# An attention and double feed-forward kernel: weight blocks placed by when their room comes free, stores in another queue, slots taken from two ends, and a new order at the end of phase one

## The chip, the cores and the metric

The kernel runs on one core of a Trainium2 chip. Five engines work side by side, each through its own instructions in order: TensorE (PE, matrix products), VectorE (DVE), ScalarE (ACT), GpSimd (POOL) and SyncE (SP, which here only issues transfers). Transfers run on 16 DMA engines and are issued from the queue of SP, ACT or POOL. The metric is the device time of one execution in microseconds (us); lower is better.

## What is computed

The input is q, k and v of 8 batches, 8 heads, 576 positions and 64 elements. Attention runs inside chunks of 64 positions; its result, 4608 tokens of 512 elements, goes through two feed-forward layers:

```python
def _moe_ref(x, w_in, w_out, g_ln):              # 512 -> 1024 -> 512
    h = x @ w_in
    h_max = np.max(h, axis=-1, keepdims=True)
    e = np.exp(h - h_max)
    sm = e / (np.sum(e, axis=-1, keepdims=True) + 1e-09)
    solu = h * sm
    mu = np.mean(solu, axis=-1, keepdims=True)
    var = np.mean((solu - mu) ** 2, axis=-1, keepdims=True)
    ln = (solu - mu) / np.sqrt(var + 1e-06) * g_ln
    return (ln @ w_out).astype(np.float32)

def _moe2_ref(x, w_in, w_out, alpha):            # 512 -> 2048 -> 512
    h = x @ w_in
    g = np.maximum(h, 0.0) + alpha * np.minimum(h, 0.0)
    return (g @ w_out).astype(np.float32)
```

## The kernel before

All arithmetic is in float32 accuracy. PE multiplies each operand as a high and a low part, so each product is three matmuls: high by high, high by low, low by high.

**Phase one** (`phase1`) does attention and the first layer on 36 tiles of 128 tokens. Its instructions stand in an order written out by hand: `FIRST`, `STEP` (repeated for each tile) and `LAST` (from line 81). In these lists `zt35` is the set of transposes of tile 35 on PE, `zh35` and `zl35` its high part (ACT) and low part (DVE), `ya31` and `yb31` the two halves of tile 31's product with `wo` on PE (24 matmuls each, lines 162 to 164), `ye31` the evacuation of that product by ACT into `ysb` and its store to DRAM (`yd`), and `sy0` to `sy7` are steps of phase two's preparation. Entries that have been done already are skipped; of `LAST`'s first line `ya30 yb30 ye29` have. The product lies in one PSUM buffer until `LAST` begins, where a second one is added, so ya31 needs ye30 out of the way; from there tiles take the two buffers in turn.

**Phase two** (`phase2`) is the second layer, with 7 products in place of 8 for a product of matrices of two by two blocks (p1 to p7 of `PRODUCTS`). Its **first half** goes through 6 groups s of 2 x 384 tokens, and in each through 8 units b, one for each weight block. A unit (class `Unit`, function `unit`) makes 7 products of 6 matmuls (line 764), adds them on DVE, applies the activation on ACT and DVE, and leaves four tiles 22, 11, 12 and 21 in g buffers, of which there are 6 for all units. `store` (line 807) sends each to DRAM (`gd`): in group 0 from POOL's queue, later from SP's. Tiles 12 and 21 of a unit are stored in the next one (`late`). A unit takes its g buffers by turns, so tile 12 of a unit takes the buffer of tile 22 of the unit before.

Weight blocks are tiles of 1.8 MB. Blocks 0 and 1 lie in a pool of the left side and are loaded during phase one. Blocks 2 to 7 lie in one pool `w2r` (line 876) on the right side, in ascending order from the address where the first layer's `wo_h` and `wo_l` lie; 2 and 3 are loaded before the first unit and 4 to 7 in units 0 to 3 of group 0 (`extra`, k = 1). In group 5 the second half's weights take their places.

The input y of a group is loaded by `load_y` (line 722) in unit 0 of the group before (at k = 3), as four tiles; `sum_y` makes four sums of them on POOL (two instructions each), at units 1 to 4, and `high_y` and `low_y` split them on ACT and DVE. These tiles lie in 26 **slots** of one pool: `slot` takes the one that has been free longest, `free` puts it back.

The **second half** goes through chunks of tokens (`CHUNKS`), each in pieces j = 0 to 3 for the products p1, p5, p6, p7 and then for p2, p3, p4. `load_g` (line 897) loads a piece from `gd` (tiles a, b, c, d), `prepare` splits it on ACT and DVE, `multiply` does 12 matmuls for each product (line 961). Pieces 0 and 1 lie in the slots of the first half (names `fa`, `fhi` and so on), later ones in a pool of their own opened behind them (`ra`, `rhi`). Piece j reads weight blocks 2j and 2j + 1, so piece 3 needs blocks 6 and 7.

Each queue issues in the order of the program: an instruction that waits holds all that stands behind it on its engine, a store or a load too.

Of the kernel before, what the change touches and what calls it, by code (L numbers as in the profile page):

```python
# [9 lines left out]
F32 = mybir.dt.float32  # L10
F32R = mybir.dt.float32r
# [22 lines left out]
SG = 384  # L34
# [8 lines left out]
def order(text):  # L43
# [36 lines left out]
)  # L80
LAST = order(
    """
    zh34 zl34 ya30 yb30 ye29 zt35 zh35 zl35 ye30 ya31 yb31 sy0 ye31 ya32 yb32 sy1 sy2 ye32 ya33 yb33 sy3 sy4
    ye33 ya34 yb34 sy5 sy6 ye34 ya35 yb35 sy7 ye35
    """
)

# [2 lines left out]
def tile_chunk_attention_solu_prelu(  # L90
# [593 lines left out]
    def phase2():  # L684
        with ExitStack() as c2:
# [4 lines left out]
            wl = P("w2l", 1)  # L690
            ps2 = [P("ps_2l", 1, space=PSUM)]
            ca = c2.enter_context(ExitStack())
            tp = P("t2", 1, stack=ca)
            up = P("u2", 1, stack=ca)
            wr = None
            W, raw, th, tl = {}, {}, {}, {}

            def load_w(b, src):
                W[b] = (wl if b < NL else wr).tile([128, 2, 7, 256], F32R, name=f"w2{b}", tag=f"w{b}")
                if src is wi_dram:  # L700
                    nc.sync.dma_start(
                        out=W[b].bitcast(F32).rearrange("p t i c -> p (t i c)"),
                        in_=src[:, b].rearrange("p t i k c -> p (t i k c)"),
                    )
                else:
                    nc.sync.dma_start(out=W[b].bitcast(F32), in_=src[:, b])

            slots = [f"y{i}" for i in range(26)]  # L710
            homes = {}

            def slot(dtype, name):
                k = slots.pop(0)
                t = tp.tile([128, 2, SG], dtype, name=name, tag=k)
                homes[t.name] = k
                return t

# [1 line left out]
                slots.append(homes.pop(t.name))  # L720

            def load_y(s):
                for t in ("11", "12", "22", "21"):
                    r, c = int(t[0]) - 1, int(t[1]) - 1
                    raw[t] = slot(F32 if t == "12" else F32R, f"y{t}")
                    nc.sync.dma_start(
                        out=raw[t].bitcast(F32), in_=y_dram[s][:, 2 * r:2 * r + 2, SG * c:SG * c + SG]
                    )

            def sum_y(k):  # L730
                out, a, b = (("t3", "22", "12"), ("t1", "12", "11"), ("t2", "22", "t1"), ("t4", "21", "t2"))[k]
                raw[out] = raw["12"] if out == "t1" else slot(F32, f"y{out}")
                for h in range(2):
                    sub(nc.gpsimd, *(raw[x][:, h].bitcast(F32) for x in (out, a, b)))

            def high_y(s, p):
                t = PRODUCTS[p][1]
                th[s, t] = slot(F32R, "th")
                copy(th[s, t], raw[t].bitcast(F32))

            def low_y(s, p):
                t = PRODUCTS[p][1]
                h, f = th[s, t], raw[t]
                l = slot(F32R, "tl") if t[0] == "t" else f
                sub(nc.vector, l, f.bitcast(F32), h.bitcast(F32))
                if t[0] == "t":
                    free(f)
                th[s, t], tl[s, t] = h, l

            class Unit:  # L750
# [54 lines left out]
                    )  # L805

                def store(self, t):
                    eng = nc.gpsimd if self.s == 0 else nc.sync
                    eng.dma_start(out=GD[t][:, self.b, self.s * SG:self.s * SG + SG], in_=self.g[t])

                def late(self, k):

# [60 lines left out]
            yield  # L873
            nal_sb = P("sm2", 1, side="right").tile([128, 48], F32, name="nal")[:, 0:KF2]
            nc.gpsimd.tensor_scalar(out=nal_sb, in0=al_sb, scalar1=-1.0, scalar2=None, op0=ALU.mult)
            wr = P("w2r", 1, side="right")
            ps2.append(P("ps_2r", 1, side="right", space=PSUM))
            gp = P("g2", 1, side="right", stack=ca)
            for b in range(NL, NL + 2):
# [5 lines left out]
            steps = [(c, g, j, p) for c in range(len(CHUNKS)) for g in range(2) for j in range(4) for p in GROUPS[g]]  # L885
            pieces = [(c, g, j) for c in range(len(CHUNKS)) for g in range(2) for j in range(4)]
            start = {x: next(t for t, y in enumerate(steps) if y[:3] == x) for x in pieces}
            src, t4s, ops = {}, {}, {}

            def new(x, tag, dtype=F32R):  # L890
                n = CHUNKS[x[0]][1]
                if x in pieces[:2]:
                    return slot(dtype, f"f{tag}")
                bufs = dict(t3=1, t2=1, t4=4, hi=4, lo=3).get(tag, 2)
                return rp.tile([128, 2, 512], dtype, name=f"r{tag}", tag=tag, bufs=bufs)[:, :, :n]

            def load_g(x):
                c, g, j = x
# [52 lines left out]
            def multiply(t):  # L951
                c, g, j, p = steps[t]
                n = CHUNKS[c][1]
                i, _, key = PRODUCTS[p]
                hi, lo = ops.pop(((c, g, j), p))
                for m in range(2):
                    if j == 0 and p not in CHAINED:
                        bank[key, m] = ps2[m].tile([128, 512], F32, name=f"o{key}", tag=f"b{key}")
                    for k in range(2):
                        for q, (a, d) in enumerate(((0, hi), (0, lo), (1, hi))):  # L960
                            nc.tensor.matmul(  # L961
                                bank[key, m][:, :n], W[2 * j + k][:, a, i, 128 * m:128 * m + 128], d[:, k],
                                start=(p not in CHAINED and j + k + q == 0), stop=(j == 3 and k == 1 and q == 2),
                                skip_group_check=True,
                            )
# [41 lines left out]


            early = {(4, 1): "p1", (5, 1): "p6", (6, 1): "p5", (7, 1): "p7", (7, 3): "p2", (8, 0): "p3", (8, 1): "p4"}
            sums = {(1, 0): 0, (2, 0): 1, (3, 0): 2, (4, 0): 3}  # L1010
            prev = None
            for s in range(NS):
                for b in range(NB2):
                    def extra(k):
                        if s == 0 and k == 1 and NL + 2 + b < NB2:
                            load_w(NL + 2 + b, wi_dram)
                        if s + 1 == NS:
                            if (b, k) == (0, 3):
                                load_g(pieces[0])
                            if (b, k) == (7, 1):  # L1020
                                load_g(pieces[1])
                            if (b, k) in ((4, 2), (5, 2), (6, 2), (7, 0)):
                                prepare(pieces[0], GROUPS[0][b - 4])
                        else:
                            if (b, k) == (0, 3):
                                load_y(s + 1)
                            if (b, k) in sums:
                                sum_y(sums[b, k])
                            if (b, k) in early:
                                high_y(s + 1, early[b, k])  # L1030
                            if (b, k - 1) in early:
                                low_y(s + 1, early[b, k - 1])
# [8 lines left out]
                        load_w(b, wo_dram)  # L1041
            for k in range(3):
                prev.late(k)
            load_w(6, wo_dram)
            for p in GROUPS[0]:
                prepare(pieces[1], p)
            for t in range(8):
                multiply(t)
            ca.close()

            rp = P("g3", 2)
            op = P("o3", 1)
            LEAD = 3
            load_g(pieces[2])
            load_w(7, wo_dram)
            load_g(pieces[3])
            for t in range(8, 8 + LEAD):
# [45 lines left out]
```

## Time and profile before

| | |
|---|---|
| time, median of 3 runs | 1335.01 us (1334.02 to 1336.84) |
| the profiled execution | 1335.51 us |
| its span in the trace | 1333.7 us |
| PE busy | 1269.7 us, 95% |
| DVE / ACT / POOL busy | 948.2 / 689.7 / 344.6 us |
| end of phase one (its last matmul starts) | 601.10 us |
| group 0 of phase two | 601.22 to 674.67 us |
| turn to the second half | about 993 us |

The span is the time from the first to the last instruction in the trace; the time contains 1.8 us around it. The clock that PE was granted is given as a share of full speed (1.00 is 2.4 GHz, 0.50 is 1.2 GHz) and is a mean over the stretch. PE is the bound, so what matters is where it stands still or runs at the lower level, and which engine, store or load it waits for there.

### The profile page before, as it was taken

What the parts mean: (1) busy time and instruction counts of PE and PEld (TensorE: products, weight loads), DVE (VectorE), ACT (ScalarE), POOL (GpSimd) and SP (SyncE); (2) the same over time, 40 slices, a digit from 0 to 9 for tenths busy, and PEclk for the clock granted to TensorE, in tenths of its full rate; (3) what the DMA queues carried; (4) which work ended last, traced back from release to release, by engine and by line L of the source; (5) the groups of instructions that cost most, each with busy time, mean ns of one, the idle gap of its engine ahead of it and who ended that gap; (6) DMA issues with size and microseconds to landing.
All of it is one profiled execution on the core that took longest, in us unless ns stands there. A gap on an engine that the chain in (4) does not pass through costs nothing. (4 is left out here: it accounts for less than half of the span.)

```text
span 1333.7 us, 21442 instructions
## 1 busy us (share of the span) xinstructions
PE 1269.7 (95%) x7968; PEld 1168.9 (88%) x7968; DVE 948.2 (71%) x1425; ACT 689.7 (52%) x1140; POOL 344.6 (26%) x343
## 2 busy tenths in 40 slices
PE   4999899999999999997999999999989999999998
PEld 3778799999898889896999999999979888888898
DVE  6996586677767677423777777777766977868584
ACT  5685355555555654423566666666544444444443
POOL 4564154354645653322340202020000000000000
PEclk9799999999999999989999999999999999999999
DMA  9774267575757563339342424426986827466362
GB/s 234 174 169 118 68 174 178 149 173 170 212 160 214 186 187 103 138 131 382 147 153 109 154 109 151 151 110 215 345 293 210 277 95 268 143 220 206 132 232 95
DMA packets 212936, 237.87 MB, mean 178 GB/s; under 512 B 89312, under 2 KB 170720, under 8 KB 210784
## 3 DMA queue, kind: packets, MB, share of 16 engines
q1 hardware_dynamic: 200832, 219.98, 53.0%
q10 hardware_dynamic: 9792, 9.44, 2.1%
q0 software_dynamic: 2208, 7.08, 1.4%
q8 instruction: 63, 1.03, 0.3%
q14 instruction: 41, 0.34, 0.1%
HBM read 149.68 MB, written 86.77 MB: 177 GB/s over the span
## 5 line engine op out<-in xcount | busy, mean ns | idle before, releaser
L162 PE MATMUL yps<-zh,wo_h 128*128 128x256 f32 x576 | 168.7, 293 | 1.6 <-ACT ysb L588 1.6
L803 DVE SCALAR_TENSOR_TENSOR g<-ng,nal,g 128x384 f32<-128x384 f32 x192 | 124.4, 648 | 62.4 <-ACT g L682 62.4
L164 PE MATMUL yps<-zh,wo_l 128*128 128x256 f32 x576 | 164.2, 285 | 0.0
L163 PE MATMUL yps<-zl,wo_h 128*128 128x256 f32 x576 | 164.1, 285 | 0.0
L682 ACT ACTIVATE ng<-g 128x384 f32<-128x384 f32 x144 | 75.7, 526 | 147.9 <-DVE g L676 147.9
L764 PE MATMUL hv<-th,w 128*128 128x384 f32 x384 | 114.6, 339 | 12.7 <-DVE g L676 12.5
L764 PE MATMUL hz<-th,w 128*128 128x384 f32 x384 | 113.6, 336 | 5.7 <-DVE wv L676 5.7
L764 PE MATMUL hx<-th,w 128*128 128x384 f32 x384 | 113.7, 336 | 0.2 <-ACT s L682 0.2
L162 PEld LDWEIGHTS yps<-zh,wo_h 128*128 128x128 f32 x576 | 111.5, 194 | 1.9 <-ACT ysb L588 1.8
L163 PEld LDWEIGHTS yps<-zl,wo_h 128*128 128x128 f32 x576 | 111.5, 194 | 0.1
L164 PEld LDWEIGHTS yps<-zh,wo_l 128*128 128x128 f32 x576 | 111.2, 193 | 0.0
L961 PE MATMUL ox<-rhi,w 128*128 128x512 f32 (+1 forms) x304 | 94.8, 373 | 0.0
L961 PE MATMUL oz<-rhi,w 128*128 128x512 f32 (+1 forms) x304 | 93.8, 369 | 0.8 <-DVE osb L676 0.8
L961 PE MATMUL ov<-rhi,w 128*128 128x512 f32 (+1 forms) x304 | 93.7, 369 | 0.0
L682 ACT ACTIVATE rhi<-rt 128x1024 fp32r<-128x1024 f32 (+1 forms) x56 | 54.7, 984 | 62.5 <-PE oz L961 16.4
L764 PEld LDWEIGHTS hv<-th,w 128*128 128x128 f32 x384 | 71.2, 189 | 15.7 <-DVE g L676 13.7
L764 PEld LDWEIGHTS hz<-th,w 128*128 128x128 f32 x384 | 70.7, 188 | 8.1 <-ACT th L682 4.9
L682 ACT ACTIVATE g<-g 128x384 f32<-128x384 f32 x144 | 75.2, 522 | 3.1
L483 PE MATMUL h<-wi_h,xh 128*128 128x512 f32 x256 | 70.9, 399 | 3.5 <-DVE sl L511 3.4
L679 DVE TENSOR_TENSOR rlo<-rt,rhi 128x1024 fp32r<-128x1024 f32 (+1 forms) x56 | 62.4, 1124 | 15.8 <-ACT rhi L682 15.5
L563 DVE TENSOR_TENSOR zl<-zt,zh 128x1024 fp32r<-128x1024 f32 x36 | 44.0, 1221 | 41.4 <-ACT zh L558 41.4
L679 POOL TENSOR_TENSOR yt<-y,y 128x384 f32<-128x384 f32 x24 | 28.1, 1192 | 169.5 <-PE hy L764 104.5
(188 smaller groups left out, 3373.0 us busy)
## 6 DMA issues: line engine op xcount, KB each, us to landing
gd<-g SPq DMA_DIRECT2D x160, 192.0 KB, 1.9
w<-wid SPq DMA_DIRECT2D x8, 1792.0 KB, 14.8
w<-wod SPq DMA_DIRECT2D x8, 1792.0 KB, 9.5
rc<-gd SPq DMA_DIRECT2D x24, 512.0 KB, 4.0
rd<-gd SPq DMA_DIRECT2D x24, 512.0 KB, 4.9
raw<-in_moe_w_out SPq DMA_DIRECT2D x24, 511.8 KB, 4.3
qt<-in_q SPq DMA_DIRECT2D x36, 256.0 KB, 5.1
kbd<-in_k SPq DMA_DIRECT2D x72, 128.0 KB, 4.9
```

The source lines that it names most:

```text
L162: nc.tensor.matmul(o, lh, rh, start=first, stop=False)
L163: nc.tensor.matmul(o, lh, rl, start=False, stop=False)
L164: nc.tensor.matmul(o, ll, rh, start=False, stop=last)
L483: nc.tensor.matmul(ps[:, n], xh[:, kk], w[:, kk, 512 * n:512 * n + 512], start=(kk == 0 and w is wi_h), stop=False,)
L563: nc.vector.tensor_tensor(out=zl, in0=ps, in1=zh.bitcast(F32), op=ALU.subtract)
L679: eng.tensor_tensor(out=out, in0=a, in1=b, op=ALU.subtract)
L682: nc.scalar.activation(out=out, in_=in_, func=func, **k)
L764: nc.tensor.matmul(self.ps[x], w[:, a, i, k], d[:, k], start=(p not in CHAINED and k + j == 0), stop=(k == 1 and j == 2), skip_group_check ...
L803: nc.vector.scalar_tensor_tensor(out=self.g[t], in0=self.n[t], scalar=nal_sb[:, f:f + 1], in1=self.g[t], op0=ALU.mult, op1=ALU.add)
L961: nc.tensor.matmul(bank[key, m][:, :n], W[2 * j + k][:, a, i, 128 * m:128 * m + 128], d[:, k], start=(p not in CHAINED and j + k + q == 0) ...
```

## The change

Six edits, of which none changes an arithmetic operation:

1. **Order at the end of phase one.** `LAST` is written anew: `zt35` stands behind yb31, `ye30` directly behind `zl34`, and the steps `sy` come in pairs, each pair a tile later.
2. **Places of the weight blocks.** In place of `w2r` there are six pools, opened from the right end in the order 2, 7, 3, 6, 5, 4; block 4 now lies lowest, over the place of `wo`, and block 2 at the right end.
3. **Slots.** Each of the 26 slots is a pool of its own. `slot` takes the lowest free one or the highest, by turns from group to group, and the highest for pieces 0 and 1.
4. **Stores.** All g stores are in SP's queue.
5. **Loads and sums of y.** `load_y` moves from unit 0 (k = 3) to unit 1 (k = 0), the first two sums from units 1 and 2 (k = 0) to unit 2 (k = 0 and 3). The tiles, the operations and the two later sums are as before.
6. **The turn.** `prepare` of piece 1 and `multiply` of piece 0 alternate, and the slots of piece 0's operands are freed behind each product. The high parts of later pieces get a pool of their own (`h3`). Block 6's load moves behind `load_g` of piece 2.

```diff
@@ LAST @@
-    zh34 zl34 ya30 yb30 ye29 zt35 zh35 zl35 ye30 ya31 yb31 sy0 ye31 ya32 yb32 sy1 sy2 ye32 ya33 yb33 sy3 sy4
+    zh34 zl34 ye30 ya31 yb31 zt35 zh35 zl35 ye31 ya32 yb32 sy0 sy1 ye32 ya33 yb33 sy2 sy3
...
@@ phase2 @@
-            tp = P("t2", 1, stack=ca)
+            tp = [P(f"t2{i}", 1, stack=ca) for i in range(26)]
             up = P("u2", 1, stack=ca)
-            wr = None
+            wr = {}
...
-                W[b] = (wl if b < NL else wr).tile([128, 2, 7, 256], F32R, name=f"w2{b}", tag=f"w{b}")
+                W[b] = (wr.get(b) or wl).tile([128, 2, 7, 256], F32R, name=f"w2{b}", tag=f"w{b}")
...
-            slots = [f"y{i}" for i in range(26)]
-            homes = {}
-
-            def slot(dtype, name):
-                k = slots.pop(0)
-                t = tp.tile([128, 2, SG], dtype, name=name, tag=k)
+            slots = list(range(26))
+            homes, at = {}, [True]
+
+            def slot(dtype, name, top=False):
+                k = slots.pop(slots.index((max if top else min)(slots)))
+                t = tp[k].tile([128, 2, SG], dtype, name=name, tag="t")
...
             def load_y(s):
+                at[0] = s % 2 == 0
                 for t in ("11", "12", "22", "21"):
                     r, c = int(t[0]) - 1, int(t[1]) - 1
-                    raw[t] = slot(F32 if t == "12" else F32R, f"y{t}")
+                    raw[t] = slot(F32 if t == "12" else F32R, f"y{t}", at[0])
...
                 def store(self, t):
-                    eng = nc.gpsimd if self.s == 0 else nc.sync
-                    eng.dma_start(out=GD[t][:, self.b, self.s * SG:self.s * SG + SG], in_=self.g[t])
+                    nc.sync.dma_start(out=GD[t][:, self.b, self.s * SG:self.s * SG + SG], in_=self.g[t])
...
-            wr = P("w2r", 1, side="right")
+
+            for b in (2, 7, 3, 6, 5, 4):
+                wr[b] = P(f"w2r{b}", 1, side="right")
...
                 if x in pieces[:2]:
-                    return slot(dtype, f"f{tag}")
+                    return slot(dtype, f"f{tag}", True)
...
-                return rp.tile([128, 2, 512], dtype, name=f"r{tag}", tag=tag, bufs=bufs)[:, :, :n]
+                return (hp if tag == "hi" else rp).tile([128, 2, 512], dtype, name=f"r{tag}", tag=tag, bufs=bufs)[:, :, :n]
...
-                hi, lo = ops.pop(((c, g, j), p))
+                hi, lo = ops0[t] = ops.pop(((c, g, j), p))
...
-            sums = {(1, 0): 0, (2, 0): 1, (3, 0): 2, (4, 0): 3}
+            sums = {(2, 0): 0, (2, 3): 1, (3, 0): 2, (4, 0): 3}
...
-                            if (b, k) == (0, 3):
+                            if (b, k) == (1, 0):
                                 load_y(s + 1)
...
-            load_w(6, wo_dram)
-            for p in GROUPS[0]:
+            for t, p in enumerate(GROUPS[0]):
                 prepare(pieces[1], p)
-            for t in range(8):
+                multiply(t)
+                free(ops0[t][0])
+                free(ops0[t][1])
+            for t in range(4, 8):
                 multiply(t)
             ca.close()
 
             rp = P("g3", 2)
             op = P("o3", 1)
+            hp = P("h3", 4)
             LEAD = 3
             load_g(pieces[2])
+            load_w(6, wo_dram)
             load_w(7, wo_dram)
             load_g(pieces[3])
```

How this moves instructions shows in three places. The first is ACT at the end of phase one, where `zh` is a high part, `ysb` an evacuation and `yd5` its store to DRAM. Before:

```order
L558 ACTIVATE zh_6406<-zt_6304 128x8x128
L558 ACTIVATE zh_6406<-zt_6410 128x8x128
L588 ACTIVATE ysb_6421<-yps_6319 128x512
L590 DMA yd5_70<-ysb_6421 128x2x256
L588 ACTIVATE ysb_6484<-yps_6424 128x512
```

Now:

```order
L558 ACTIVATE zh_6481<-zt_6304 128x8x128
L588 ACTIVATE ysb_6485<-yps_6319 128x512
L590 DMA yd5_70<-ysb_6485 128x2x256
L558 ACTIVATE zh_6481<-zt_6537 128x8x128
L588 ACTIVATE ysb_6548<-yps_6488 128x512
```

Tile 30's evacuation has changed places with the high part of tile 35.

The second is the start of group 0 in SP's queue; `w22` to `w27` are weight blocks 2 to 7, `y11` to `y21` the next group's input, and `gd3`, `gd0`, `gd1`, `gd2` take the tiles 22, 11, 12, 21. Before:

```order
L701 DMA w22_6743<-wid_71 128x3584
L701 DMA w23_6745<-wid_71 128x3584
L701 DMA w24_6767<-wid_71 128x3584
L726 DMA y11_6788<-yd1_66 128x2x384
L726 DMA y12_6790<-yd1_66 128x2x384
L726 DMA y22_6792<-yd1_66 128x2x384
L726 DMA y21_6794<-yd1_66 128x2x384
L701 DMA w25_6859<-wid_71 128x3584
L701 DMA w26_6942<-wid_71 128x3584
L701 DMA w27_7026<-wid_71 128x3584
```

Now:

```order
L701 DMA w24_6857<-wid_71 128x3584
L809 DMA gd3_76<-g_6873 128x384
L809 DMA gd0_73<-g_6884 128x384
L727 DMA y11_6927<-yd1_66 128x2x384
L727 DMA y12_6929<-yd1_66 128x2x384
L727 DMA y22_6931<-yd1_66 128x2x384
L727 DMA y21_6933<-yd1_66 128x2x384
L809 DMA gd1_74<-g_6895 128x384
L809 DMA gd2_75<-g_6909 128x384
L701 DMA w25_6946<-wid_71 128x3584
L809 DMA gd3_76<-g_6962 128x384
```

Blocks 2 and 3 stand ahead of block 4 as before; the stores have come in between the loads. In POOL's queue they stood between the sums (`yt3`, then `y12` and so on). Before:

```order
L809 DMA gd3_76<-g_6783 128x384
L809 DMA gd0_73<-g_6802 128x384
L679 TENSOR_TENSOR yt3_6845<-y22_6792,y12_6790 128x384 x2
L809 DMA gd1_74<-g_6813 128x384
L809 DMA gd2_75<-g_6827 128x384
L809 DMA gd3_76<-g_6875 128x384
L809 DMA gd0_73<-g_6886 128x384
L679 TENSOR_TENSOR y12_6790<-y12_6790,y11_6788 128x384 x2
```

Now POOL has only the sums there:

```order
L875 TENSOR_SCALAR nal_6807<-al_sb_62 128x16
L679 TENSOR_TENSOR yt3_7016<-y22_6931,y12_6929 128x384 x2
L679 TENSOR_TENSOR y12_6929<-y12_6929,y11_6927 128x384 x2
L679 TENSOR_TENSOR yt2_7102<-y22_6931,y12_6929 128x384 x2
L679 TENSOR_TENSOR yt4_7186<-y21_6933,yt2_7102 128x384 x2
```

All of group 0's stores are gone from it.

The third is SP's queue at the turn, from the last store of the first half on; `ra` to `rd` are the tiles of a piece, first those of piece 2. Before:

```order
L809 DMA gd2_75<-g_10809 128x384
L706 DMA w26_10818<-wod_72 128x3584
L902 DMA ra_10956<-gd0_73 128x2x384
L902 DMA rb_10958<-gd1_74 128x2x384
L902 DMA rc_10960<-gd3_76 128x2x384
L902 DMA rd_10962<-gd2_75 128x2x384
L706 DMA w27_10964<-wod_72 128x3584
L902 DMA ra_10966<-gd0_73 128x2x384
```

Now:

```order
L809 DMA gd2_75<-g_10899 128x384
L904 DMA ra_11072<-gd0_73 128x2x384
L904 DMA rb_11074<-gd1_74 128x2x384
L904 DMA rc_11076<-gd3_76 128x2x384
L904 DMA rd_11078<-gd2_75 128x2x384
L706 DMA w26_11080<-wod_72 128x3584
L706 DMA w27_11082<-wod_72 128x3584
L904 DMA ra_11084<-gd0_73 128x2x384
```

Piece 2 stands ahead of block 6, and both blocks stand between pieces 2 and 3.

## Rows read from the trace of the kernel before

**Rows 1.** The page: the span, and busy time of each engine.
```profile
span 1333.7 us, 21442 instructions
...
PE 1269.7 (95%) x7968; PEld 1168.9 (88%) x7968; DVE 948.2 (71%) x1425; ACT 689.7 (52%) x1140; POOL 344.6 (26%) x343
```

**Rows 2.** Stretches: us, PE, PEld, DVE, ACT, POOL busy (count), clock, DMA share, GB/s.
```profile
560.00:580.00 20.00, 16.44 (x114) 16.00 (x113) 5.09 (x9) 5.71 (x9) 8.58 (x10) 0.83 0.75 290
...
620.00:640.00 20.00, 12.10 (x56) 11.47 (x54) 5.78 (x11) 5.00 (x12) 9.86 (x14) 0.74 0.95 389
...
980.00:1000.00 20.00, 14.71 (x83) 14.39 (x82) 11.38 (x13) 4.47 (x7) 0.54 (x1) 0.89 0.88 324
```

**Rows 3.** PE's timeline, phase one's end: start, us, engine, line, operation [idle before <-releaser].
```profile
561.83 0.28 PE L164 MATMUL yps<-zh,wo_l 128*128 128x256 f32 x1
...
564.71 0.28 PE L164 MATMUL yps<-zh,wo_l 128*128 128x256 f32 x1
566.95 1.09 PE L545 MATMUL zt<-ident,sl 128*128 128x128 f32 x8 [1.96 <-DVE zl L563]
569.64 0.58 PE L162 MATMUL yps<-zh,wo_h 128*128 128x256 f32 x1 [1.60 <-ACT ysb L588]
```

**Rows 4.** ACT's timeline at the same place: zh34, zh35, and the evacuation of tile 30.
```profile
564.00 1.00 ACT L558 ACTIVATE zh<-zt 128x1024 fp32r<-128x1024 f32 x1
568.08 1.02 ACT L558 ACTIVATE zh<-zt 128x1024 fp32r<-128x1024 f32 x1 [3.07 <-PE zt L545]
569.00 0.59 ACT L588 ACTIVATE ysb<-yps 128x512 f32<-128x512 f32 x1
```

**Rows 5.** PE's timeline: first matmuls of groups 0 to 3, and two gaps.
```profile
601.22 0.34 PE L764 MATMUL hx<-th,w 128*128 128x384 f32 x1
...
632.30 0.69 PE L764 MATMUL hv<-th,w 128*128 128x384 f32 x1 [7.90 <-DVE g L676]
...
674.67 0.33 PE L764 MATMUL hx<-th,w 128*128 128x384 f32 x1
...
734.67 0.33 PE L764 MATMUL hx<-th,w 128*128 128x384 f32 x1
...
740.68 0.41 PE L764 MATMUL hz<-th,w 128*128 128x384 f32 x1 [0.64 <-DVE wv L676]
...
794.09 0.33 PE L764 MATMUL hx<-th,w 128*128 128x384 f32 x1
```

**Rows 6.** DVE's timeline: waits for stores in groups 0 and 5; a pass at the turn.
```profile
631.69 0.56 DVE L676 TENSOR_TENSOR g<-hv,wv 128x384 f32<-128x384 f32 x1 [9.14 <-DMA gd<-g]
...
940.71 0.56 DVE L676 TENSOR_TENSOR g<-hv,wv 128x384 f32<-128x384 f32 x1 [0.86 <-DMA gd<-g]
...
995.69 0.96 DVE L679 TENSOR_TENSOR rt<-rc,rb 128x768 f32<-128x768 f32 x1 [7.11 <-DMA rc<-gd]
```

**Rows 7.** POOL's timeline in group 0: the first sum.
```profile
623.02 1.97 POOL L679 TENSOR_TENSOR yt<-y,y 128x384 f32<-128x384 f32 x2 [13.18 <-DMA y<-yd]
```

**Rows 8.** SP's waits, 540 to 700 (total, times, longest); y loads of 598 to 640, to landing.
```profile
SPq L701 <- PE yps L164: 34.8, 1, 34.8
...
DMA to landing us min/median/max: 16.9/18.1/19.5
```

**Rows 9.** SP's timeline at the turn: issues of block 6 and of piece 2's first tile.
```profile
980.33 0.48 SPq L706 DMA_DIRECT2D w<-wod  x1
988.65 0.37 SPq L902 DMA_DIRECT2D ra<-gd  x1
```

**Rows 10.** PE's timeline at the turn: the gap, and the end of the slow stretch.
```profile
998.82 0.69 PE L961 MATMUL ox<-ra,w 128*128 128x384 f32 x1 [5.29 <-DVE ra L679]
...
1002.47 0.33 PE L961 MATMUL oz<-rhi,w 128*128 128x384 f32 x1
```

**Rows 11.** Issue to landing: g stores of POOL (600 to 650), then of SP (930 to 976).
```profile
DMA to landing us min/median/max: 2.1/6.6/12.0
...
DMA to landing us min/median/max: 2.0/5.7/10.4
```

More of the change, by code (lines that the diff above doesn't have):

```diff
@@ L82 @@
     """
-    zh34 zl34 ya30 yb30 ye29 zt35 zh35 zl35 ye30 ya31 yb31 sy0 ye31 ya32 yb32 sy1 sy2 ye32 ya33 yb33 sy3 sy4
-    ye33 ya34 yb34 sy5 sy6 ye34 ya35 yb35 sy7 ye35
+    zh34 zl34 ye30 ya31 yb31 zt35 zh35 zl35 ye31 ya32 yb32 sy0 sy1 ye32 ya33 yb33 sy2 sy3
+    ye33 ya34 yb34 sy4 sy5 ye34 ya35 yb35 sy6 sy7 ye35
     """
@@ L731, in sum_y @@
                 out, a, b = (("t3", "22", "12"), ("t1", "12", "11"), ("t2", "22", "t1"), ("t4", "21", "t2"))[k]
-                raw[out] = raw["12"] if out == "t1" else slot(F32, f"y{out}")
+                raw[out] = raw["12"] if out == "t1" else slot(F32, f"y{out}", at[0])
                 for h in range(2):
@@ L737, in high_y @@
                 t = PRODUCTS[p][1]
-                th[s, t] = slot(F32R, "th")
+                th[s, t] = slot(F32R, "th", at[0])
                 copy(th[s, t], raw[t].bitcast(F32))
@@ L743, in low_y @@
                 h, f = th[s, t], raw[t]
-                l = slot(F32R, "tl") if t[0] == "t" else f
+                l = slot(F32R, "tl", at[0]) if t[0] == "t" else f
                 sub(nc.vector, l, f.bitcast(F32), h.bitcast(F32))
@@ L887, in phase2 @@
             start = {x: next(t for t, y in enumerate(steps) if y[:3] == x) for x in pieces}
-            src, t4s, ops = {}, {}, {}
+            src, t4s, ops, ops0 = {}, {}, {}, {}
             def new(x, tag, dtype=F32R):
```

## Prediction

> **What bounds the kernel now.** I read the page first: TensorE (PE) is busy for nearly the whole span [rows 1], so time can only come from its idle gaps and from stretches at the lower of its two clock levels (1.2 and 2.4 GHz). The busy table by stretch shows where they are: 560 to 580 us has a granted clock of 0.83 and PE busy 16.44 us of 20; 620 to 640 has 0.74 and 12.10; 980 to 1000 has 0.89 and 14.71 [rows 2]. Between them PE is full or nearly so. The three places are the end of phase one (A), the first group of phase two (B) and the turn from its first half to its second (C). The change touches all three.
>
> In A the PE timeline shows two gaps, 1.96 us before the transposes of tile 35 and 1.60 us before tile 31's product; the second ends on ScalarE's (ACT) evacuation `ysb` [rows 3]. ACT's timeline says why: `ysb` of tile 30 stands behind the copy `zh35`, which waits for those transposes [rows 4]. In B PE waits 7.90 us for a VectorE (DVE) addition, and DVE had waited 9.14 us until a store `gd<-g` gave a g buffer back [rows 5, 6]. The store was late because GpSimd (POOL), whose queue it was in, sat 13.18 us at a sum that needs the next group's y [rows 7]. That y landed 16.9 to 19.5 us after its issue, in the queue of SyncE (SP) behind weight blocks 2 to 4, and the first of those had waited 34.8 us for the last matmul of phase one [rows 8]. In C PE waits 5.29 us for `ra`'s low part, issued at 988.65 behind weight block 6 (980.33) [rows 9, 10].
>
> **A, the new order.** Before: yb30's last matmul starts at 564.71 and lasts 0.28, so 564.99; phase two's first matmul starts at 601.22 [rows 3, 5]. That is 36.23 us. Five tiles of 48 matmuls remain and one set of transposes. At full clock matmuls follow each other every 0.12 us (561.83 to 564.71 is 24 steps) [rows 3], so 5 x 5.76 = 28.8 us, and 1.09 us for the transposes. Now `ysb` of tile 30 follows `zh34`, which ends at 565.00, and takes 0.59 [rows 4]; with 0.1 us to signal, ya31 starts near 565.7, 0.7 us after yb30. The sum is 0.7 + 28.8 + 1.1 = 30.6, a gain of 5.6 us: 2.8 of idle time and 2.8 that the half-clock stretch cost. The transposes now run behind yb31, their input long ready; ACT and DVE have two tiles of PE work to split tile 35, and ye31 has until ya33. The halving followed two gaps close together; one of 0.7 us should not bring it (a group with a gap of 0.64 us kept its pace, 59.42 us [rows 5]), but if it does, 2.8 us return. Range 3 to 6.
>
> **B, weight places, stores, sums.** Unit starts on PE give the groups: group 0 ran from 601.22 to 674.67, 73.45 us; group 1 to 734.67, 60.00; group 2 to 794.09, 59.42, of which 0.64 is one gap that only a group behind another has [rows 5]. An undisturbed group 0 is 59.42 - 0.64 = 58.8, group 1 59.4: at most 14.65 + 0.6 = 15.2 us to win. What the edits do to that:
> - Places. Blocks 2 and 3 no longer lie over `wo`; as built they wait for tile 33's last product, two tiles (11.5 us) before phase one's end; block 4 still waits for the last. 3.7 MB leave the rush behind 601.
> - Stores in SP's queue. SP's order becomes block 4, two stores, the four y loads, two stores, block 5, four stores, block 6, four stores, block 7. No sum stands before a store. Issue on SP costs nothing on PE's path. A buffer is wanted again about one unit (59.42 / 8 = 7.4 us) and two products after its store's issue, some 9 us. With T the start of group 0: block 4 (1.84 MB at 353 to 389 GB/s, I take [rows 2]'s 389) is through by T+5, before the first store; y (1.57 MB) from T+8 to T+13; block 5 to T+18.5; unit 1's first store lands near T+19.5 and is wanted at T+21.3. Blocks 6 and 7 leave similar slack, about 2 us.
> - The bounds: below, no wait at all, 15.2 gained. Above, stores on POOL beside the rush took a median of 6.6 us and up to 12.0 to land; on SP beside weight loads, in the last group, 5.7 and up to 10.4 [rows 11], and there DVE waited 0.86 us for one [rows 6]. The last group is the nearest row: it does with six blocks what group 0 will do with three. I take that wait plus 0.4 for DVE slowed by the sums on POOL: 14.0 gained. Range 8 to 15.2.
>
> The rule that speaks against this part is in the Trainium skill, "DMA: Bandwidth & Descriptors", section "Queues, rings and completion order": a DMA engine takes one ring's descriptors in order and alternates between rows that have work. By it a POOL store could slip past SP's weight bytes and an SP store cannot, so the move would cost landing time; the trace shows the opposite sign, 5.7 against 6.6 us, though under different loads. By the rule B comes out as in rival 1, near 7.5; by the row it is the 14.0.
>
> In groups 1 to 4 the y load moves behind two of unit 0's stores and the sums from unit 1 to unit 2. The products from y are wanted from unit 4 on, so nothing waits; I cost it at nothing, 0 to 0.5 us each way. Slots from both ends and phase two's pools only decide what a load must wait for.
>
> **C, the turn.** Now piece 2's loads stand before block 6, and their slots are released by unit 47 and by piece 0's own landings, not by piece 0's products. They can be issued at about 980.4 (times of the old trace), when block 6 was [rows 9], and 1.57 MB at 324 GB/s [rows 2] is 4.9 us. ACT and DVE then have some eight microseconds; PE wanted it at 998.82 - 5.29 = 993.5 [rows 10], so the 5.29 us go. Behind the gap eleven matmuls took 998.82 to 1002.47, 3.65 us [rows 10], where full clock gives 1.9 (58.8 us for a group's 336 matmuls are 0.175 each), so some 1.7 more go: 7.0 at most. What is late next: blocks 6 and 7 (3.67 MB) now stand between piece 2 and piece 3. At 324 GB/s they end near 997 to 998, piece 3's a, b, c near 1001, and its low part needs three DVE passes of 0.96 us [rows 6], to near 1004, while PE, started on time, wants it 48 matmuls later, at 993.5 + 8.4 = 1001.9. About 2 us of new idle: 5.0 gained. Range 2 to 7.
>
> **Sum.** 5.6 + 14.0 + 5.0 = 24.6 us. The profiled execution took 1335.51 us with a span of 1333.7; it becomes 1310.9 with a span of 1309.1. It stood 0.5 above the median of 1335.01, so I predict **1310.4 us**.
>
> **Rivals.**
> 1. *Stores stuck in SP's queue.* The slack of 2 us is small. If the DMA engines give 300 instead of 389 GB/s, or y starts 3 us later, blocks 5, 6 and 7 each push a store past its time by 2 to 3 us. For it: landing maxima above 10 us [rows 11]. Against: only 0.86 us in the last group. B falls to 7.5: 1316.9. Chance 0.17.
> 2. *The turn stays bound by data.* Piece 3 arrives later than I have it, since block 7 must also wait for the DMA engines; C gives 2: 1313.4. Chance 0.12.
> 3. *The blocks are not released early.* If a wait on the last matmul still holds blocks 2 and 3, the rush stays, and stores on SP stand behind 5.5 MB as y did (18.1 us [rows 8]), twice the 9 us that a buffer has; B falls to 5 or 6: 1319. Chance 0.06.
> 4. *Slower.* One mechanism: in groups 0 to 4 the y load now stands between unit 0's first two and last two stores. If it waits there for a slot, or its bytes take long, four g buffers stand still and PE with them. The 24.6 us are eaten from 4.9 us lost in each of five groups. A store has 9 us and the load's bytes take 4 to 5, so it would have to hold the queue for about 14 us, for example for slots freed only in unit 1 or 2. At 6 us lost in each: 30 - 24.6 = 5.4 over, 1340.4. Nothing in the rows shows such a wait. Chance 0.05.
>
> **How the numbers follow.** The forecast has 0.60: 1310.4, its own range 1305 to 1316. The range reaches over rivals 1 and 2 and takes in most of 3: 1304.5 to 1319.5; its lower end is all three upper bounds (28.2) and a little of the later groups' 0.64. What a measurement can tell from no change is 0.2%, 2.7 us. Forecast and rivals 1 to 3 are all faster (0.95); rival 4 gives slower 0.035, and 0.015 where it only eats the gain.
>
> **What would show it.** A: no PE gap over 1 us and a granted clock of 1.00 from 560 to 600. B: no PE gap over 2 us in group 0, its length 59 to 61 us; gaps released by a store at units 2 to 4 would be rival 1. C: no gap at piece 2's start, one of some 2 us at piece 3's. Wrong would be a new half-clock stretch anywhere, or groups 1 to 4 longer than 59.4.

## The result, and the profile after

| | before | after |
|---|---|---|
| time, median | 1335.92 us (1334.02 to 1338.08, 4 runs) | 1316.38 us (1314.03 to 1318.95, 4 runs) |
| ratio after / before, 95% interval | | 0.9854 [0.9829, 0.9878] |
| span of the profiled execution | 1333.7 us | 1314.6 us |

The change gains 19.5 us where 24.6 were forecast; the time lies inside the stated range, 6.0 us above the forecast. The page of after, its first lines (span, busy time by engine):

```profile
span 1314.6 us, 21447 instructions
...
PE 1264.9 (96%) x7968; PEld 1165.5 (89%) x7968; DVE 951.4 (72%) x1425; ACT 689.4 (52%) x1140; POOL 328.1 (25%) x311
```

The stretches that answer to [rows 2] (columns as there: PE, PEld, DVE, ACT, POOL busy, clock, DMA share, GB/s):

```profile
560.00:580.00 20.00, 19.31 (x162) 19.11 (x161) 7.42 (x11) 6.90 (x10) 9.03 (x10) 1.00 0.80 306
...
600.00:620.00 20.00, 20.00 (x117) 20.00 (x116) 13.30 (x23) 9.99 (x22) 8.41 (x8) 1.00 0.95 341
620.00:640.00 20.00, 19.88 (x115) 19.55 (x114) 15.41 (x29) 13.31 (x28) 0.37 (x1) 1.00 0.75 276
...
980.00:1000.00 20.00, 15.55 (x74) 15.23 (x73) 13.15 (x18) 7.41 (x10) 0.00 (x0) 0.83 0.52 175
```

The first two places are mended: clock 1.00 and PE full. The third is not. The stretch 980 to 1000 of after is some 20 us later in the work than that of before, and it again has a low clock and a PE that stands still. PE's timeline in after shows where (start, us, operation, idle before and what ended it):

```profile
566.73 0.38 PE L162 MATMUL yps<-zh,wo_h 128*128 128x256 f32 x1 [0.69 <-ACT ysb L588]
...
596.49 0.34 PE L765 MATMUL hx<-th,w 128*128 128x384 f32 x1
...
655.16 0.33 PE L765 MATMUL hx<-th,w 128*128 128x384 f32 x1
...
976.19 0.44 PE L963 MATMUL oz<-rlo,w 128*128 128x384 f32 x1 [0.51 <-DVE rlo L679]
...
987.17 0.69 PE L963 MATMUL ox<-ra,w 128*128 128x384 f32 x1 [4.45 <-DVE ra L679]
```

The two gaps at phase one's end [rows 3] have become one of 0.69 us. Group 0 runs from 596.49 to 655.16, 58.67 us against 73.45 [rows 5], with no gap above 0.2 us. At the turn piece 2 starts on time, but piece 3 waits 4.45 us where piece 2 waited 5.29 [rows 10].

Phase one's part ahead of the edited lists is the same in all kernels, yet in the profiled executions its end (yb30's last matmul) lies anywhere between 561.9 and 569.1 us. So times are compared with their intervals, and the parts of the change by stretches inside one trace. The ratios are to runs of before that were taken together with each kernel; their medians lie between 1335.92 and 1338.42 us, so times in us from different sections are not compared directly. In this table "end of phase one" runs from yb30's end to phase two's first matmul, "turn" from the matmul behind the gap of 1.0 us in the last unit (974.34 before, 954.34 after) to the first matmul that waits for an output tile `osb` (1045.77 and 1026.72).

| kernel | end of phase one | group 0 | group 1 | turn | time, ratio to before |
|---|---|---|---|---|---|
| before | 36.23 | 73.45 | 60.00 | 71.43 | 1 |
| after | 30.45 | 58.67 | 59.42 | 72.38 | 0.9854 [0.9829, 0.9878] |
| o1: order alone | 30.45 | 72.59 | 60.04 | 71.56 | 0.9948 [0.9931, 0.9964] |
| g1: stores alone | 35.82 | 66.33 | 59.42 | 72.28 | 0.9938 [0.9914, 0.9962] |
| g2: places alone | 35.81 | 64.38 | 59.77 | 72.03 | 0.9930 [0.9905, 0.9955] |
| g3: after, stores back | 30.46 | 63.60 | 59.66 | 72.01 | 0.9881 [0.9850, 0.9912] |
| g4: after, places back | 30.45 | 66.60 | 59.42 | 72.00 | 0.9876 [0.9853, 0.9899] |
| y1: after, y load back | 30.46 | 58.24 | 59.42 | 71.10 | 0.9837 [0.9822, 0.9852] |
| t1: after, block 6 first | 30.45 | 58.86 | 59.42 | 69.27 | 0.9817 [0.9792, 0.9843] |
| t2: after, block 6 in the middle | 30.45 | 58.84 | 59.42 | 69.22 | 0.9815 [0.9793, 0.9837] |
| t3: after, blocks 6 and 7 in the middle | 30.45 | 58.56 | 59.87 | 71.13 | 0.9835 [0.9813, 0.9857] |
| t4: after, oldest slot | 30.45 | 58.79 | 59.56 | 78.36 | 0.9892 [0.9872, 0.9912] |
| t5: block 6 early | 30.45 | 58.91 | 59.42 | 67.89 | 0.9818 [0.9805, 0.9831] |
| t6: block 6 and piece 1 early | 30.45 | 58.96 | 59.49 | 66.52 | 0.9821 [0.9796, 0.9847] |

From before to after the stretches give 5.78 + 14.78 + 0.58 - 0.95 = 20.2 us; phase one's front took 1.05 us more in the profiled execution of after (yb30 ends at 566.04 against 564.99), which leaves the 19.1 us between the spans. How well a turn repeats shows in the table: the four kernels with the old turn (before, o1, g1, g2) have 71.4 to 72.3 us, the four with the new one (after, g3, g4, y1) 71.1 to 72.4. A difference of less than some 1.3 us says nothing there.

### The profile page after: what moved, and what is told of

Same layout as the page of the kernel before. It is cut to its first block, busy times and chain, and to the rows that moved or that the text cites. A ratio compares the mean times of both kernels' runs of the same rounds, so it can differ in the third digit from the quotient of the medians.

```text
span 1314.6 us, 21447 instructions
## 1 busy us (share of the span) xinstructions
PE 1264.9 (96%) x7968; PEld 1165.5 (89%) x7968; DVE 951.4 (72%) x1425; ACT 689.4 (52%) x1140; POOL 328.1 (25%) x311
```

## Experiments

### The turn: three orders of the loads, and the slots

The question is where the 5 us went that piece 2's earlier start should have brought. SP's timeline in after (start, us, line, load):

```profile
961.44 0.53 SPq L904 DMA_DIRECT2D rc<-gd  x1
966.18 0.36 SPq L904 DMA_DIRECT2D rd<-gd  x1
966.59 0.94 SPq L706 DMA_DIRECT2D w<-wod  x2
967.58 0.46 SPq L904 DMA_DIRECT2D ra<-gd  x1
...
969.12 0.60 SPq L904 DMA_DIRECT2D rc<-gd  x1
```

SP stands for 4.2 us (961.97 to 966.18) at piece 2's fourth load, with both blocks and piece 3 behind it. SP's waits (line, cause, total, times, longest) put 3.9 us of that on DVE's subtraction `ft`, which still uses the slot:

```profile
SPq L904 <- DVE ft L679: 3.9, 1, 3.9
```

Right behind that wait the DMA engines run dry. Their rate in 40 slices of 0.75 us from 955 to 985 in after:

```profile
GB/s 182 195 342 375 395 328 375 395 391 293 219 283 356 377 293 55 57 92 382 451 418 437 492 363 459 421 440 459 382 459 401 342 371 395 384 356 371 373 371 373
```

The three slices of 55, 57 and 92 GB/s run from 966.25 to 968.5. Then the engines are full to the end, and piece 3's third tile lands 14.9 us after its issue. DVE's timeline in after shows what follows, three passes up to PE's 987.17:

```profile
984.10 0.96 DVE L679 TENSOR_TENSOR rt<-rc,rb 128x768 f32<-128x768 f32 x1 [6.22 <-DMA rc<-gd]
985.09 0.96 DVE L679 TENSOR_TENSOR rb<-rb,ra 128x768 f32<-128x768 f32 x1
986.15 0.96 DVE L679 TENSOR_TENSOR ra<-ra,rhi 128x768 fp32r<-128x768 f32 x1
```

Two causes are possible, the queue that stood still or the sheer bytes.

**t1, block 6 first.**

```diff
+            load_w(6, wo_dram)
             load_g(pieces[2])
-            load_w(6, wo_dram)
             load_w(7, wo_dram)
```

> The changed kernel with one line put back: block 6's load stands in front of piece 2's loads again; all else as changed. In the changed kernel piece 2 started on time, but the gap came back at piece 3 (4.45 us, released by ra's low part), with 0.51 us before it and a half-clock stretch from 987.17 to 993.3 behind it. Theory (idle queue): SP stood from 961.44 to 966.18 at piece 2's fourth load, which waits for a slot, with both blocks behind it, while the DMA engines ran down to 239 GB/s. Block 6 in front fills that time: piece 3 comes 4 to 5 us earlier, its gap falls below 1 us, and a gap of at most 1.5 us opens at piece 2; the time falls by 5 to 7 us to 1309 to 1311. Rival (bytes): pieces 2 and 3 and two blocks are 6.8 MB, which cannot be there in time in any order; the gap moves to piece 2 and stays 3 to 5 us; 1314 to 1317.

Measured: 1312.03 us (1310.02 to 1316.49), turn 69.27, 3.1 us less than after and 1.8 less than the shortest turn with after's order (y1, 71.10). PE's timeline in t1 has one gap left, at piece 2:

```profile
976.49 0.44 PE L963 MATMUL ox<-ra,w 128*128 128x384 f32 x1 [3.35 <-DVE ra L679]
```

Piece 3 has none. Both theories are half right: the engines no longer run dry (no microsecond from 961 to 970 is below 262 GB/s) and the turn is shorter, but the gap moved to piece 2 as the bytes' side said, and the time, as a ratio too, is a little above the 1309 to 1311 of the first theory. Since t1 differs from after in nothing but block 6's place, this also says which part of the change at the turn was the loss: the rest of the change, the slots above all (t4, below), shortens the turn by some 2 to 3 us, and moving block 6 behind piece 2's loads gives that back.

**t2, block 6 in the middle; t3, both blocks in the middle.** In `load_g`, in front of tile d of piece 2:

```diff
+                    if x == pieces[2] and tag == "d":
+                        load_w(6, wo_dram)
```

t3 has the same with `load_w(7, wo_dram)` behind it; the lines at the turn are taken out.

> The changed kernel with block 6's load between piece 2's third and fourth load (ra, rb, rc, block 6, rd, block 7). Theory (idle queue): SP issues block 6 at about 962 instead of 966.6 and has work in the DMA engines while it waits for rd's slot; piece 2 is as early as in the changed kernel (no gap), piece 3 is 4 us earlier, gap below 1 us; 1309 to 1311. Rival (bytes): piece 3's gap stays above 3 us; 1314 to 1317.

> The changed kernel with blocks 6 and 7 both between piece 2's third and fourth load. Theory (idle queue): as with block 6 alone for piece 3, but rd now comes behind 3.7 MB and lands near 974 to 975, where DVE wants it at 974.3; gap of 0 to 1 us inside piece 2, below 1 us at piece 3; 1309 to 1312. Rival (bytes): piece 3's gap above 3 us; 1314 to 1317.

Measured: t2 1312.77 us (1309.57 to 1314.36), turn 69.22; t3 1315.31 us (1313.55 to 1315.87), turn 71.13. The gaps in t2, on PE's timeline:

```profile
975.46 0.44 PE L965 MATMUL oz<-rlo,w 128*128 128x384 f32 x1 [0.60 <-DVE rlo L679]
...
984.10 0.44 PE L965 MATMUL ox<-ra,w 128*128 128x384 f32 x1 [2.10 <-DVE ra L679]
```

And in t3, PE's gap:

```profile
979.85 0.69 PE L966 MATMUL oz<-rlo,w 128*128 128x384 f32 x1 [4.66 <-DVE rlo L679]
```

and the wait on DVE's timeline that made it:

```profile
977.96 0.96 DVE L679 TENSOR_TENSOR rt<-rd,rt 128x768 f32<-128x768 f32 x1 [3.67 <-DMA rd<-gd]
```

t2 halves piece 3's gap and t3 closes it, but in t3 tile d of piece 2 lands behind both blocks and opens a gap of 4.66 us there; the 0 to 1 us expected for it was wrong, and t3's turn cannot be told from after's. Both times are above those expected. In all three orders the DMA engines move 333 to 440 GB/s in every 5 us from 960 to 980, and gaps of 2.7 to 4.7 us stay. So some 2 to 3 us of after's loss go with the idle queue (t1, t2). That the rest is bytes is so far argued from the full engines: none of the three orders removes it, and others were not tried. t5 and t6, below, take bytes out.

**t4, the oldest free slot.**

```diff
-                k = slots.pop(slots.index((max if top else min)(slots)))
+                k = slots.pop(0)
```

> The changed kernel with slots taken as before, the one that has been free longest, in place of the lowest or highest by turns; places, order, queues as changed. Theory: the turns of the slots only decide what a load at the turn waits for; if this is what lets piece 2's loads go at 960, they now wait for later work, and the turn loses up to 3 us; groups 0 to 4 do not change; 1316 to 1320. Rival: the slots do nothing measurable: 1315 to 1317 and the same gaps within 0.3 us.

Measured: 1323.1 us (1320.38 to 1324.06), turn 78.36, 6.0 us more than after; twice what was expected. SP's timeline in t4, its first load of piece 2:

```profile
966.43 0.37 SPq L904 DMA_DIRECT2D ra<-gd  x1
```

and PE's two gaps there:

```profile
976.58 0.69 PE L963 MATMUL ox<-ra,w 128*128 128x384 f32 x1 [5.30 <-DVE ra L679]
990.88 0.69 PE L963 MATMUL ox<-ra,w 128*128 128x384 f32 x1 [3.81 <-DVE ra L679]
```

The load goes 14.4 us behind the start of the turn (952.04), in after 6.0 us behind it (960.38 against 954.34); piece 2 waits as in the kernel before, and piece 3 waits too. SP's long wait is again the one for DVE's `flo`, 8.4 us in t4 and 7.7 in before. So the new choice of slots is what lets piece 2's loads go. The run undoes the whole choice, the turns from group to group and the highest slot for pieces 0 and 1, and does not tell which of the two it is.

### Group 0: each part alone, and each undone

**g1, the stores alone**, in the kernel before:

```diff
-                    eng = nc.gpsimd if self.s == 0 else nc.sync
-                    eng.dma_start(out=GD[t][:, self.b, self.s * SG:self.s * SG + SG], in_=self.g[t])
+                    nc.sync.dma_start(out=GD[t][:, self.b, self.s * SG:self.s * SG + SG], in_=self.g[t])
```

> The kernel before with one edit alone: the g stores of group 0 in SP's queue. The y load stays in unit 0 ahead of them, the weight blocks stay where they were. Group 0 took 73.45 us before and 58.7 us in the changed kernel. Theory (POOL's sum is the plug): without the sum in front the stores go at once and land behind 5.5 MB of weights and 1.6 MB of y, some 20 us after phase one's end; group 0 falls to 63 to 67 us. Rival (queue): a store in SP's queue behind weights and y is as late as it was behind the sum; group 0 stays at 72 to 76 us.

**g2, the places alone**, in the kernel before:

```diff
-            wr = P("w2r", 1, side="right")
+            for b in (2, 7, 3, 6, 5, 4):
+                wr[b] = P(f"w2r{b}", 1, side="right")
```

> The kernel before with one edit alone: six pools for the weight blocks, in the order 2, 7, 3, 6, 5, 4 from the right end. Stores stay in POOL's queue behind the sums. Theory (rush): blocks 2 and 3 are loaded during the last two tiles of phase one, y lands some 10 us after its issue in place of 18, the sum goes at about 614 in place of 623, and group 0 falls to 61 to 66 us. Rival (plug alone): group 0 stays above 70 us because the stores still stand behind the sum.

Measured: g1 1328.65 us (1327.24 to 1329.97), group 0 66.33 us, 7.1 less than before; g2 1327.41 us (1326.0 to 1329.45), group 0 64.38, 9.1 less. Both as their theories had it. In g1, DVE still waits once for a store that stood behind weights and y (issued at 606.33, landed 15.1 us later):

```profile
621.52 0.56 DVE L676 TENSOR_TENSOR g<-hz,u 128x384 f32<-128x384 f32 x1 [5.85 <-DMA gd<-g]
```

In g2, POOL's first sum waits 2.50 us for y and not 13.18 [rows 7], and PE's largest gap, through DVE and ACT, is 2.70 (POOL's timeline, then PE's):

```profile
611.65 1.98 POOL L679 TENSOR_TENSOR yt<-y,y 128x384 f32<-128x384 f32 x2 [2.50 <-DMA y<-yd]
```

```profile
630.18 0.45 PE L764 MATMUL hx<-th,w 128*128 128x384 f32 x1 [2.70 <-ACT s L682]
```

**g3, the stores put back, in the kernel after** (the two lines of g1, the other way round).

> The changed kernel with one part undone: group 0's stores in POOL's queue again. Theory (it is the rush and the time of the sums that count): y has landed before POOL comes to the first sum in unit 2, no store waits for it, and group 0 stays within 1 us of 58.7; the time stays at 1314 to 1319. Rival (SP's queue is needed): the sums hold the stores again and group 0 is 3 us longer or more.

Measured: 1322.15 us (1318.84 to 1323.67), group 0 63.60, 4.9 more than after. The theory fell: y had landed before the first sum, and yet SP's queue is needed. The rival has the outcome but not the mechanism, since no sum held a store: POOL sat idle, waiting for DVE or to issue, before each store of group 0 there. SP's timeline in g3:

```profile
597.47 2.20 SPq L727 DMA_DIRECT2D y<-yd  x4
599.71 7.01 SPq L701 DMA_DIRECT2D w<-wid  x3
```

and in after:

```profile
604.64 2.00 SPq L727 DMA_DIRECT2D y<-yd  x4
...
607.83 0.73 SPq L701 DMA_DIRECT2D w<-wid  x1
...
615.74 0.45 SPq L701 DMA_DIRECT2D w<-wid  x1
...
623.70 0.42 SPq L701 DMA_DIRECT2D w<-wid  x1
```

With no store among them, blocks 5 to 7 go out within 7 us (block 7 at 606.3), ahead of or beside the first four stores (604.02 to 607.90), which are wanted first. In after each block waits its turn behind the stores of a unit. Issue to landing of these four stores, in g3 and then in after:

```profile
DMA to landing us min/median/max: 7.4/10.9/12.1
```

```profile
DMA to landing us min/median/max: 1.8/4.0/6.2
```

The same of all g stores of 595 to 645, in g3 (POOL's queue):

```profile
DMA to landing us min/median/max: 2.1/3.4/12.1
```

and in after (SP's queue):

```profile
DMA to landing us min/median/max: 1.8/4.7/9.1
```

The median of all is better on POOL, but not that of the first stores, and one of them is what DVE waits for longest, 3.08 us in g3; it was issued at 605.02 and landed 10.6 us later:

```profile
615.69 0.56 DVE L676 TENSOR_TENSOR g<-hv,u 128x384 f32<-128x384 f32 x1 [3.08 <-DMA gd<-g]
```

Once block 7 has landed (626.2), a store in POOL's queue takes 2.2 us (the one issued at 626.80). So the traces say that the blocks sent early are what made the first stores late. No run has POOL's stores with the blocks issued at after's times, so this cause is read from the traces and not shown by an experiment.

**g4, the places put back, in the kernel after.**

```diff
-            for b in (2, 7, 3, 6, 5, 4):
-                wr[b] = P(f"w2r{b}", 1, side="right")
+            w2r = P("w2r", 1, side="right")
+            for b in range(NL, NB2):
+                wr[b] = w2r
```

> The changed kernel with one part undone: blocks 2 to 7 in one pool in ascending order, so that block 2 lies over wo again and is loaded at phase one's end. Stores stay in SP's queue. Theory (rush): the first stores stand behind 5.5 MB and land some 15 us into group 0, just when their buffers are wanted; the later ones behind y; group 0 grows by 3 to 9 us; the time is 1319 to 1326. Rival (places do nothing): group 0 stays within 1 us of 58.7.

Measured: 1320.45 us (1319.09 to 1321.51), group 0 66.60, 7.9 more than after, as the theory had it. SP issues blocks 2 to 4 from 592.56, 0.2 us behind phase two's first matmul (592.37), where after has the first of them 11.4 us ahead of it (585.09, 596.49), and DVE waits for stores (SP's timeline, then DVE's):

```profile
592.56 1.27 SPq L701 DMA_DIRECT2D w<-wid  x3
```

```profile
621.55 0.56 DVE L676 TENSOR_TENSOR g<-hz,u 128x384 f32<-128x384 f32 x1 [2.66 <-DMA gd<-g]
```

### The order at the end of phase one, and the y load

**o1, the order alone**: `LAST` of the change in the kernel before.

> The kernel before with one edit alone: the new order at the end of phase one. From yb30's end to phase two's first matmul took 36.2 us before and 30.45 in the changed kernel. Theory (own gain): the stretch falls to 30.5, group 0 keeps its 73.4 us, the time falls by 5.8 us (ratio 0.9957). Rival (given back): y and the stores hang on the last matmul and on each other, and group 0 grows by what phase one gave, to 76 us or more; ratio 0.998 to 1.000.

Measured: 1331.72 us (1328.27 to 1333.5); 30.45 us at phase one's end, group 0 72.59. The stretch gives what it gives in after, and nothing comes back later: the gap of 7.90 us in group 0 [rows 5] is still 7.04. PE's timeline in o1:

```profile
569.06 0.38 PE L162 MATMUL yps<-zh,wo_h 128*128 128x256 f32 x1 [0.69 <-ACT ysb L588]
...
629.06 0.69 PE L764 MATMUL hv<-th,w 128*128 128x384 f32 x1 [7.04 <-DVE g L676]
```

**y1, the y load and the sums put back, in the kernel after.**

```diff
-            sums = {(2, 0): 0, (2, 3): 1, (3, 0): 2, (4, 0): 3}
+            sums = {(1, 0): 0, (2, 0): 1, (3, 0): 2, (4, 0): 3}
...
-                            if (b, k) == (1, 0):
+                            if (b, k) == (0, 3):
```

> The changed kernel with one part undone: the y load in unit 0 (ahead of its first two stores) and the first two sums at units 1 and 2 as before. Theory: y's 1.6 MB stand before two stores that have some 9 us to spare, and in group 0 block 4 stands before y; group 0 grows by 0 to 2 us, groups 1 to 4 stay at 59.4; 1315 to 1319. Rival (the move matters): y in front delays the first stores past their time, group 0 is 3 us longer or more.

Measured: 1316.42 us (1314.21 to 1318.88); group 0 58.24 and group 1 59.42, against 58.67 and 59.42. This part of the change is worth nothing that these runs show. It also clears y in g3: in both kernels the y loads go 0.6 us behind the start of group 0 and land in a median of 9.3 us, and y1, with the blocks behind the stores, loses nothing.

### Bytes taken out of the turn

The three orders left the bytes. Block 6 can go earlier: its place is free when unit 6 of the last group is done, as those of blocks 0 to 5 are one unit at a time.

**t5 and t6**, both with block 6 loaded right behind unit 6 and out of the turn:

```diff
-                    if s + 1 == NS and b < 6:
+                    if s + 1 == NS and b < 7:
                         load_w(b, wo_dram)
...
             load_g(pieces[2])
-            load_w(6, wo_dram)
             load_w(7, wo_dram)
```

t5 moves piece 1's loads from (7, 1) to (7, 0), in front of unit 6's last two stores; t6 moves them to (6, 3), in front of block 6.

> The changed kernel with block 6 loaded as soon as unit 6 of the last group is done, as blocks 0 to 5 are, and piece 1's loads one step earlier, in front of unit 6's last two stores. With block 6 at the turn the DMA engines were full from 955 to 980 in all three orders tried, and 2.7 to 4.7 us of gaps stayed in the turn. Theory (bytes): what helps is to take 1.8 MB out of that stretch; block 6 goes at about 950, where the share is below 1, piece 1 may be up to 1.5 us late, pieces 2 and 3 are on time; gaps in the turn below 2 us, no half-clock stretch, 1307 to 1310. Rival (order of slots): the early load shifts the slots, rc now waits for piece 0's products and the gap moves to piece 2 or 1: 1312 to 1317.

> The changed kernel with block 6 as in the run beside it, and piece 1's loads in unit 6 (behind its 7th part of 3 steps, ahead of its stores) so that they stand before block 6. Theory (bytes): piece 1 is early, block 6 goes at about 951, pieces 2 and 3 on time; gaps in the turn below 1.5 us, but unit 6's stores go 4 us later and a gap at units 6 and 7 of the last group may grow by 1 to 2 us; 1306 to 1310. Rival: the later stores cost 3 us or more, 1312 to 1316.

Measured: t5 1313.83 us (1313.22 to 1314.83), turn 67.89; t6 1313.96 us (1308.89 to 1317.82), turn 66.52, 5.9 less than after and 4.9 less than before. The gaps of units 4 to 7 did not grow, and the clock stayed at 1.00 from 955 to 995 in both; but both times are above those expected. t6 has one gap in the turn, which follows from a wait of DVE (PE's timeline, then DVE's):

```profile
981.19 0.44 PE L963 MATMUL oz<-rlo,w 128*128 128x384 f32 x1 [2.26 <-DVE rlo L679]
```

```profile
978.31 0.96 DVE L679 TENSOR_TENSOR rt<-rc,rb 128x768 f32<-128x768 f32 x1 [3.63 <-DMA t4d<-ft]
```

The wait is now for the store of piece 1's `ft` to DRAM, in whose place the next pool's `rt` lies; in after the same pass waited 1.18 us for it. t5 has the same wait, 3.02 us. In t6 PE and DVE wait for no load in the turn. But the store took 9.1 us to land, while the DMA engines moved 352 GB/s at a busy share of 0.97, so bytes may still be behind this gap; no run tests that. Against the 69.2 us of the best order t6's 66.5 lies beyond the scatter of 1.3 us, and t5's 67.9 just at it: taking block 6 out of the turn gave more than the three orders did. By the profile t6 is the best of all kernels here; by the times the ratios of t1, t2, t5 and t6 (0.9815 to 0.9821) cannot be told apart, and their intervals touch that of after.

## Why the prediction was right, point by point

- **A, forecast 5.6 us, came to 5.78**, alone as well as with the rest. One gap of 0.69 us and a clock of 1.00 from 560 to 600, as worked out.
- **B, forecast 14.0, came to 14.78 + 0.58 = 15.4**, all that the rows allowed. Group 0 runs without a wait for a store, in 58.67 us; the wait of 0.86 us and the 0.4 us that the forecast kept did not come. Stores and places were both needed: alone they gave 7.1 and 9.1, undone they cost 4.9 and 7.9. The prediction saw SP's order only as a risk, a store behind a block; g3's trace points to the other side, a block held back behind the stores. The Trainium skill's rule ("DMA: Bandwidth & Descriptors", "Queues, rings and completion order") that was weighed against this part, by which stores on POOL could slip past the weights, fits g3's median of 3.4 us against 4.7, and not the first four stores, 7.4 to 12.1 us against 1.8 to 6.2, which are what made the time. The prediction took the trace's side, and that was right, but its figure was thinner than it says: the median of 5.7 us [rows 11] counts three loads of piece 0 along with the stores, and the stores alone have 6.2, against 6.6 on POOL.
- **C, forecast 5.0, came to -0.95**, and since old and new turns both scatter by about 1 us, it is best read as no gain. This is the step that failed, by 6 us; A and B together gave 1.5 us more than forecast. Its first half held: piece 2 was issued at 960.38 and started without a gap. The mis-sized term was "piece 3's a, b, c near 1001". In times of the old trace (20.0 us later) they landed at 1004, since the loads behind tile d stood still with it and the DMA engines ran dry for 2.3 us. The prediction took all of piece 2's loads as issued at once and overlooked what the fourth one waits for: its place is that of piece 1's `ft`, not free until DVE is done with it at about 966. The second omission was the clock. The forecast had 2 us of new idle time and nothing behind it; the idle time was 4.45 + 0.51, and the 18 matmuls from 987.17 to 993.10 took 5.93 us, at a granted clock of 0.50, where full clock (0.175 each) gives 3.15, 2.8 more. Together 7.8 us against the 7.0 that were to be won. A new half-clock stretch was what the prediction itself had named as a sign of being wrong.
- **The rivals.** The second (turn bound by data) is nearest to what happened, harder than it was priced (a gain of 2) and in part by another cause: it has piece 3 late because block 7 waits for the DMA engines, and 2 to 3 us of it were SP's wait. The first (stores stuck) and the third (blocks not released early) did not: block 2 was issued at 585.09, 11.4 us before group 0. The fourth (the y load holds the stores) did not either: group 1 stayed at 59.42, and y1 shows that where this load stands does not matter.
- **The sum.** 1310.4 was missed by C, and 1316.38 lies 0.4 us outside the forecast's own 1305 to 1316. The whole range, 1304.5 to 1319.5, held because it reached to rivals 1 and 2; that the time came out next to rival 1's 1316.9 is chance, since B was whole. What was right for its reasons is A and B, 19.6 of the 24.6 us.

## What to carry to other kernels

A queue that is taken in order is also a pace: a large load that is not wanted yet is best put behind the small transfers that are. Here the stores' queue was worth 4.9 us (undone) to 7.1 us (alone) of group 0, and the earlier places 7.9 to 9.1 us. Before moving a group of loads up, ask of each one what it waits for, because one that waits holds all that stand behind it. When a stall is removed, price the next one with its half-clock stretch. When several orders of the same loads leave gaps while the DMA engines are full, stop ordering and move bytes to a stretch with room.

## What the runs showed of the hardware that was not expected

After SP's wait at 966.18 the DMA engines stayed below 100 GB/s for 2.25 us, though four loads had been issued by 968.1; then they went to 382 and above. And gaps of like size left the clock differently: t6's 2.26 us left it at 1.00, t5's of 2.08 us too, and t2's 2.10 us, with one of 0.60 that ended 8.6 us earlier, was followed by 0.70. The stretches with the granted clock, t6 and then t2 (columns as above):

```profile
980.00:985.00 5.00, 3.81 (x22) 3.81 (x23) 4.83 (x7) 1.64 (x4) 0.00 (x0) 1.00 1.05 368
```

```profile
985.00:990.00 5.00, 5.00 (x23) 5.00 (x22) 4.48 (x5) 3.21 (x6) 0.00 (x0) 0.70 0.74 220
```

Why they differ these runs do not settle.
